# Key weights first on a second DMA queue, value weights fourth on the first, engine lists reordered and most filler matmuls dropped

The kernel is one pre-norm transformer block (linear attention, then a gated feed-forward), in bfloat16. It runs on one core of a Trainium2 chip. The metric is the device time of one execution in microseconds (us). Executions of one kernel differ: the kernel before took 208.06 to 208.45 us in its first four (0.2%). Names such as `wT`, `w2m`, `pp` and `vv` are those of the operations in the kernel's own order lists; PE is TensorE, DVE is VectorE, ACT is ScalarE, POOL is GpSimd, SP is SyncE.

## The reference

```python
# x: (1, 2048, 448), 16 heads of 28; everything bfloat16
def _A_ref(x, wqkv, w_phi, wo):
    qkv = (x @ wqkv).reshape(B, S, 3, H, Dh).transpose(2, 0, 3, 1, 4)
    q, k, v = qkv[0], qkv[1], qkv[2]
    pq = einsum("bhsd,hdf->bhsf", q, w_phi)
    pk = einsum("bhsd,hdf->bhsf", k, w_phi)
    phi_q = concatenate([softmax(pq), softmax(-pq)], -1)
    phi_k = concatenate([softmax(pk), softmax(-pk)], -1)
    kv = einsum("bhsf,bhsd->bhfd", phi_k, v)
    ...                                   # num, den, o = num / den
    return o.reshape(B, S, D) @ wo
h  = x + _A_ref(layernorm(x), wqkv, w_phi, wo)
h2 = h + (sigmoid(n @ w_gate) * (n @ w_up)) @ w_down        # n = layernorm(h)
```

`k` is only used through `w_phi`, so the kernel multiplies the key weights by `w_phi` once (the "fold": transpose the key weights on PE, `wT`; evacuate, that is, copy the result out of PE's accumulator; multiply, `w2m`; evacuate) and then projects x with the product (`pp`). The value projection (`vv`) needs no fold. `kv` is a sum over all 16 row tiles of x, so nothing after it can start before all tiles are through.

## The kernel before

Each engine runs a list of named operations in a fixed order; semaphores make an operation wait for what it reads. The order lists are the tuned part. The loads of the opening:

```python
def load(name, dst, src, w, kb, r=(), eng="sp"):
    return op(eng, name, lambda e: e.dma_start(dst, src), r=r, w=w, dma="in" if eng == "sp" else "ain", ...)
op("dve", "bd0", lambda e: e.memset(Wphi[:], 0.0), w=["Wphi"])
def kload(a, b):                                    # key weights, two halves of 196 KB
    load("ld_k%d" % a, wk_sb[:, a:b, :], A_wqkv[a * GP:b * GP, D:2 * D]..., (b - a) * 98)
for hl in range(4):                                 # w_phi: four loads into a block diagonal
    load("wphi%d" % hl, Wphi[hl * DH:(hl + 1) * DH, :, hl * DH:(hl + 1) * DH],
         A_w_phi...[hl], [("Wphi", hl)], 6, r=["Wphi"], eng="act")
# matmuls on zeros ("fillers"; "warm" in the lists): (how many, columns)
for i, (n, size) in enumerate(((9, 512), (1, 128), (5, 128), (1, 128), (8, 128), (9, 128), (9, 128), (3, 128))):
    op("pe", "warm%d" % i, warm(n, size), r=["zero"], w=[B(3)])
ORDER = {
  "sp":  "x1 x0 ld_k0 x2 ld_k2 x4 x6 ld_v0 x10 ld_v2 ld_q2 x8 ... xT12 xT13 xT14 ld_woo1 xT15 ld_wd0 ld_woe0 ld_wu2 ...",
  "act": "wphi3 wphi2 wphi1 wphi0 wTe1 wTe0 wTe3 w2e0_0 ...",
  "pe":  "warm0 wT1 wT0 warm1 xT1 warm2 xT0 warm3 wT2 wT3 w2m0_0 warm4 w2m0_1 w2m0_3 w2m0_2 warm5 xT2 warm6 "
         "ppa0 warm7 ppb0 xT3 vva0 vvb0 ppa2 ...",
  ...
}
```

Here `x1` and so on load tiles of x, `xT4` to `xT15` are DMA transposes of normalised tiles, `ld_wg`, `ld_wu`, `ld_wd`, `ld_wo` are the later weights.

The softmax here doesn't subtract the row's maximum and nothing guards it: scores larger than these inputs give would overflow.

Of the kernel before, what the change touches and what calls it, by code (L numbers as in the profile page):

```python
# [18 lines left out]
class Graph:  # L19
# [86 lines left out]
    def emit(self, nc):  # L106
# [94 lines left out]

ORDER = {
    "sp": (
        "x1 x0 ld_k0 x2 ld_k2 x4 x6 ld_v0 x10 ld_v2 ld_q2 x8 ld_q3 ld_q1 ld_q0 xT4 xT5 xT6 x14 x12 xT7 ld_woe1 xT8 "
        "xT9 xT10 xT11 xT12 xT13 xT14 ld_woo1 xT15 ld_wd0 ld_woe0 ld_wu2 ld_wg0 ld_wg2 ld_wd1 ld_wg3 ld_wu3 ld_woo0 "
        "ld_wu0 ld_wg1 ld_wd4 ld_wd6 ld_wu1 oT3 oT2 oT4 oT5 oT6 oT7 hT2 ld_wd3 ld_wd2 hT3 ld_wd5 hT4 oT8 oT9 hT5 hT6 "
        "hT7 oT11 oT10 oT12 out3 out1 hT9 hT8 oT13 hT11 hT10 oT14 oT15 out5 hT12 hT14 out2 hT15 out4 hT13 out9 out7 "
        "out10 out6 out14 out0 out15 out12 out11 out8 out13 "
    ),
    "act": (  # L210
        "wphi3 wphi2 wphi1 wphi0 wTe1 wTe0 wTe3 w2e0_0 w2e0_1 w2e0_2 w2e0_3 xn3 xn4 ek0 ek1 xn5 v1_0 v1_1 xn6 ek2 ek3 "
        "v1_2 w2e1_1 v1_3 xn7 ek4 w2e1_3 xn9 w2e1_2 ek5 v1_5 v1_6 ek6 xn11 ek7 xn12 ek8 v1_8 xn13 ek9 xn14 ek10 v1_10 "
        "ek11 v1_11 ek12 v1_12 ek13 v1_13 ek14 eq0_0 ek15 v1_14 v1_15 eq0_1 eq1_0 eq1_1 eq2_0 oT0e eq2_1 sq0 sq1 "
        "eq3_0 eq3_1 sig0_1 sig0_0 sig0_3 sig0_2 sig0_5 sig0_4 sig0_7 sq2 sig0_6 sq3 sig0_9 sig0_8 sig0_10 sig0_11 "
        "sq5 sig0_12 sig0_13 sq4 sq7 sig2_0 sig2_1 sq6 sig2_3 sig2_2 sig2_5 sig2_4 sig2_6 sig2_7 sig2_8 sig2_9 "
        "sig2_10 sig2_11 sig2_12 sig2_13 sig4_1 sq9 sig4_0 sig4_3 sq8 sig4_2 sig4_5 sig4_4 sig4_7 sig4_6 sig4_9 sq10 "
        "sig4_8 sq11 sig4_11 sig4_10 sig4_13 sig4_12 sig8_1 sig8_0 sq13 sig8_2 sig8_3 sig8_4 sig8_5 sq12 sig8_6 sq14 "
        "sq15 sig8_7 sig8_9 sig8_8 sig8_10 sig8_11 sig8_13 sig8_12 sig12_0 sig12_1 sig12_3 sig12_2 sig12_5 sig12_4 "
        "sig12_7 sig12_6 sig12_8 sig12_9 sig12_11 sig12_10 sig12_12 sig12_13 "
    ),  # L220
    "pe": (
        "warm0 wT1 wT0 warm1 xT1 warm2 xT0 warm3 wT2 wT3 w2m0_0 warm4 w2m0_1 w2m0_3 w2m0_2 warm5 xT2 warm6 ppa0 warm7 "
        "ppb0 xT3 vva0 vvb0 ppa2 ppb2 vva2 vvb2 kva0 w2m1_1 w2m1_0 kvb0 kva1 pva4 kvb1 pvb4 w2m1_3 w2m1_2 pva5 pva6 "
        "pvb5 pvb6 kva2 pqa0_0 kvb2 pva7 kva3 pvb7 pva8 kvb3 pvb8 pva9 kva4 pvb9 kvb4 pva10 kva5 pvb10 pva11 kvb5 "
        "kva6 pvb11 kvb6 pva12 kva7 pvb12 pva13 kvb7 pvb13 kva8 pva14 kvb8 kva9 pvb14 kvb9 pqb0_0 kva10 pva15 kvb10 "
        "kva11 pvb15 kvb11 kva12 pqa0_1 kvb12 kva13 pqb0_1 kvb13 kva14 pqa1_0 kvb14 kva15 kvb15 pqb1_0 pqa1_1 num0 "
        "num1 pqb1_1 pqa2_0 pqb2_0 num2 pqa2_1 oT0 pqb2_1 oT1 num3 woa0 wob0 pqa3_0 num4 pqb3_0 pqa3_1 pqb3_1 num5 "
        "hT0 hT1 ga0_1 gb0_1 ga0_0 num6 gb0_0 ga0_3 woa2 gb0_3 ga0_2 wob2 gb0_2 num7 ga0_5 gb0_5 ga0_4 gb0_4 ga0_7 "
        "gb0_7 ga0_6 num8 gb0_6 woa4 ga0_9 ga0_8 gb0_9 gb0_8 wob4 ga0_11 ga0_10 gb0_11 gb0_10 woa6 num9 wob6 ga0_13 "
        "ga0_12 gb0_13 gb0_12 dn0_0 dn0_4 ga2_0 ga2_1 gb2_0 gb2_1 dn0_8 dn0_11 ga2_3 num10 ga2_2 gb2_3 dp0_0 gb2_2 "  # L230
        "dp0_4 ga2_5 ga2_4 gb2_5 gb2_4 dp0_8 dp0_11 ga2_6 ga2_7 gb2_6 gb2_7 woa8 ga2_8 ga2_9 gb2_8 gb2_9 wob8 num11 "
        "ga2_10 ga2_11 gb2_10 gb2_11 dn2_0 ga2_12 ga2_13 gb2_12 gb2_13 dn2_4 dn2_8 ga4_1 num12 gb4_1 ga4_0 dn2_11 "
        "gb4_0 dp2_0 ga4_3 ga4_2 gb4_3 dp2_4 num13 gb4_2 ga4_5 dp2_8 gb4_5 ga4_4 dp2_11 gb4_4 ga4_7 num14 gb4_7 ga4_6 "
        "woa10 gb4_6 ga4_9 wob10 gb4_9 ga4_8 num15 gb4_8 ga4_11 woa12 gb4_11 ga4_10 wob12 gb4_10 ga4_13 dn4_0 ga4_12 "
        "gb4_13 gb4_12 dn4_4 ga8_1 ga8_0 gb8_1 gb8_0 dn4_8 dn4_11 ga8_3 ga8_2 dp4_0 gb8_2 dp4_4 dp4_8 gb8_3 ga8_4 "
        "dp4_11 gb8_4 ga8_5 woa14 gb8_5 ga8_6 wob14 gb8_6 ga8_7 dn6_0 gb8_7 dn6_4 ga8_8 ga8_9 dn6_8 gb8_9 gb8_8 "
        "dn10_0 dn6_11 ga8_11 ga8_10 gb8_11 gb8_10 dp6_0 dp6_4 dp6_8 ga8_13 ga8_12 gb8_13 gb8_12 dp6_11 dn10_4 dn10_8 "
        "ga12_0 ga12_1 gb12_0 dn8_0 dn10_11 gb12_1 ga12_2 dp10_0 ga12_3 dn8_4 gb12_3 gb12_2 dp10_4 dn8_8 ga12_5 "
        "dn8_11 ga12_4 gb12_5 gb12_4 dp8_0 dp8_4 ga12_7 ga12_6 gb12_7 dp10_8 dp10_11 gb12_6 dp8_8 dp8_11 ga12_9 "
        "ga12_8 gb12_9 gb12_8 dm14_0 dm12_0 dm15_0 ga12_11 ga12_10 gb12_11 gb12_10 dm12_4 dm14_4 dm13_0 ga12_12 "  # L240
        "ga12_13 gb12_12 gb12_13 dm15_4 dm14_8 dm15_8 dm12_8 dm15_10 dm14_10 dm14_12 dm14_13 dm15_12 dm12_10 dm12_12 "
        "dm15_13 dm12_13 dm13_4 dm13_8 dm13_10 dm13_12 dm13_13 "
    ),
    "dve": (
        "zero bd0 bst1 agg1 bst0 agg0 ve1_0 nm1_0 nm1_1 xn1 bst2 bst3 agg2 agg3 ve1_3 xT0e wTe2 bst5 nm1_3 bst4 agg5 "
        "agg4 bst6 xT1e ve1_4 bst7 agg7 agg6 bst10 xT2e bst11 agg10 xT3e nm1_6 ss0 agg11 rs0 ss1 bst8 rs1 bst9 agg8 "
        "ss2 agg9 ss3 w2e1_0 rs3 rs2 v1_4 bst15 bst14 bst13 ss4 agg14 agg13 bst12 rs4 agg15 agg12 xn10 ss5 ss6 v1_7 "
        "rs6 rs5 ss7 rs7 ss8 v1_9 ss9 rs9 rs8 xn15 ss10 ss11 rs11 rs10 ss12 rs12 ss13 phi11 ss14 rs13 rs14 phi13 ss15 "
        "rs15 phi15 kvz1 kvz0 rsm0 qq0 rsm1 b0 c0 qq1 den0 b1 rden0 c1 rsm2 den1 qq2 rden1 b2 c2 den2 oT1e rsm3 rden2 "
        "qq3 b3 c3 h0 den3 nm0 rden3 h1 rsm4 nm1 qq4 b4 c4 den4 hn0 hn1 rsm5 hT0e hT1e qq5 b5 c5 den5 rden4 hh0_1 "  # L250
        "rsm6 qq6 rden5 b6 hh0_0 c6 den6 rden6 hh0_3 h2 rsm7 hh0_2 qq7 b7 hh0_5 c7 nm2 hh0_4 den7 rden7 h3 nm3 rsm8 "
        "hh0_7 hh0_6 hn2 qq8 b8 hn3 hh0_9 hh0_8 h5 h4 nm5 c8 nm4 den8 hh0_10 hh0_11 rsm9 qq9 h6 h7 b9 c9 hh0_12 "
        "hh0_13 nm7 rden8 nm6 den9 hh2_0 hh2_1 hn4 rsm10 rden9 qq10 b10 hh2_3 c10 hh2_2 hn6 hn7 den10 hh2_5 hh2_4 "
        "fin0 fin1 hh2_6 hh2_7 hn5 rden10 hh2_8 hh2_9 h8 h9 hh2_10 hh2_11 rsm11 qq11 nm9 b11 hh2_13 c11 hh2_12 den11 "
        "rsm12 qq12 nm8 b12 c12 rden11 hh4_1 hh4_0 o10 den12 hh4_3 rsm13 qq13 b13 rden12 hh4_2 c13 hh4_5 den13 fin3 "
        "hn9 rden13 hh4_4 hn8 fin2 rsm14 hh4_7 o13 qq14 b14 c14 hh4_6 den14 h10 h11 nm10 hh4_9 nm11 rsm15 hn10 hh4_8 "
        "hn11 hh4_11 qq15 h13 h12 hh4_10 b15 c15 hh4_13 nm13 hh4_12 den15 nm12 rden15 o15 rden14 hh8_1 hh8_0 o14 "
        "hh8_2 hh8_3 fin4 fin5 hh8_4 hh8_5 h15 h14 nm14 hh8_6 nm15 hn12 hn14 hh8_7 hh8_9 hh8_8 hn13 hn15 hh8_11 "
        "hh8_10 hh8_12 hh8_13 fin6 fin7 hh12_0 hh12_1 hh12_3 hh12_2 hh12_5 hh12_4 hh12_7 fin11 hh12_6 fin9 fin10 fin8 "
        "hh12_8 hh12_9 hh12_11 hh12_10 hh12_12 hh12_13 fin14 fin15 fin12 fin13 "  # L260
    ),
    "pool": (
        "ident0 phipad wqpad mask0 neghalf ident ve1_1 pow1_1 pow1_0 xn0 v1ones mask1 nm1_2 ve1_2 pow1_2 nb1_2 xn2 "
        "pow1_3 nm1_4 nb1_3 pow1_4 nb1_4 ve1_6 opad0 mask2 pow1_6 nb1_6 phi0 phi1 nm1_8 ve1_8 pow1_8 nb1_8 xn8 phi2 "
        "phi3 ve1_12 nm1_12 pow1_12 kvzones nb1_12 phi4 phi5 phi6 phi7 phi8 phi9 phi10 phi12 phi14 o0 o1 o2 o3 ve0 "
        "pow2_0 ve1 pow2_1 o4 o5 o6 o7 ve2 pow2_2 ve3 pow2_3 ve5 ve4 pow2_4 o8 pow2_5 ve7 o9 ve6 pow2_7 pow2_6 ve8 "
        "ve9 o11 pow2_9 o12 pow2_8 ve10 pow2_10 ve11 pow2_11 ve12 pow2_12 ve14 pow2_14 ve15 ve13 pow2_15 pow2_13 "
    ),
}
PROGRAM = (  # L270
    "pq:0,0,4 pq:0,1,4 kvz pq:1,0,0 pq:1,1,4 pq:2,0,0 num:0 num:1 ot:0 ot:1 wo:0 pq:2,1,4 pq:3,0,0 num:2 num:3 "
    "wo:2 pq:3,1,4 gu:0,2 num:4 num:5 wo:4 gu:2,2 num:6 num:7 wo:6 down:0,2 num:8 num:9 wo:8 down:2,2 num:10 "
    "num:11 wo:10 gu:4,4 num:12 num:13 wo:12 down:4,2 num:14 num:15 wo:14 down:6,2 gu:8,4 down:8,2 down:10,6 "
    "gu:12,4 down1:12,2 down1:13,3 down1:14,6 down1:15,7 "
)



def windows(ap):
# [26 lines left out]
def build(nc, A_x, A_wqkv, A_w_phi, A_wo, B_w_gate, B_w_up, B_w_down, out):  # L306
# [10 lines left out]
    with ExitStack() as es:  # L317
# [3 lines left out]
        ident = sb("ident", [P, P])  # L321
        zero = sb("zero", [P, 512])
        neghalf = sb("neghalf", [P, 4], f32)
# [100 lines left out]

        def kload(a, b):
            load("ld_k%d" % a, wk_sb[:, a:b, :], A_wqkv[a * GP:b * GP, D:2 * D].rearrange("(kt p) n -> p kt n", p=GP),
                 [("wk", kt) for kt in range(a, b)], (b - a) * 98)

        def vload(k):
            r0 = ROW0[k]  # L430
            load("ld_v%d" % k, wv_sb[:, k:k + 2, :], A_wqkv[r0:r0 + 256, 2 * D:3 * D].rearrange("(kt p) n -> p kt n", p=P),
                 [("wv", k), ("wv", k + 1)], 224)
        kload(0, 2)
        kload(2, 4)
        for hl in range(4):
# [28 lines left out]
                    p = e.matmul(bk(3)[:, 0:size], lhsT=zero[:, 0:P], rhs=zero[:, 0:size], start=True, stop=True)  # L464
                return p
            return f
        for i, (n, size) in enumerate(((9, 512), (1, 128), (5, 128), (1, 128), (8, 128), (9, 128), (9, 128), (3, 128))):
            op("pe", "warm%d" % i, warm(n, size), r=["zero"], w=[B(3)])

        def evac(name, dst, src, rkey, wkey):  # L470
# [64 lines left out]
        for kt in range(KT):  # L535
            b = (0, 1, 4, 5)[kt]
# [351 lines left out]
```

## Time and profile before

| | before |
|---|---|
| time, median (lowest to highest) | 208.24 us (208.06 to 208.45, 4 runs) |
| PE busy, share of the span | 96% |
| first real projection (`ppa0`) starts | 10.59 us |
| `kv` sum masked (`kvz`, on DVE) starts | 46.27 us |

The first lines of the page give the span and each engine's busy time.

```profile
span 206.8 us, 5794 instructions
...
PE 199.2 (96%) x2457; PEld 112.6 (54%) x2457; DVE 136.6 (66%) x343; ACT 95.2 (46%) x185; POOL 59.0 (29%) x99
```

PE is busy 96% of the time, so it bounds the kernel; but part of that is work on zeros. The chain of waits, followed back from the end (start, length, what), says where the opening comes from.

```profile
2.17 3.85 DMA x_sb<-in_A_x_dram
...
9.76 0.40 PE psum L478 x4
10.16 0.50 PE psum L464 x9
10.66 0.86 PE psum L289 x8
```

It starts at a load of x (the tiles `x2`), and nine fillers stand in the chain at 10.16 us. The timeline of the opening (start, length, engine, line, operation, then in brackets how long the engine had been idle and what ended it) has the first statistics of x, the fold, fillers around it, and the first projection.

```profile
2.88 0.63 DVE L485 BATCH_NORM_STATS2 st<-x_sb 128x6 f32<-128x448 bf16 x1 [1.46 <-DMA x_sb<-in_A_x_dram]
...
6.54 0.52 PE L464 MATMUL psum<-zero 128*128 128x128 bf16 x5
...
7.59 0.36 PE L553 MATMUL psum<-Wphi,WkT 112*128 112x112 bf16 x4
...
7.79 0.61 PE L464 MATMUL psum<-zero 128*128 128x128 bf16 x8
...
9.99 0.67 PE L464 MATMUL psum<-zero 128*128 128x128 bf16 x9
...
10.59 0.93 PE L289 MATMUL psum<-Wk,xnT 64*128 64x448 bf16 x8
```

DVE's timeline of the kernel before, at `kvz`, in the same columns:

```profile
46.27 1.19 DVE L657 TENSOR_TENSOR kvz<-psum,maskK 120x464 bf16<-120x464 f32 x2 [1.01 <-PE psum L289]
```

### The profile page before, as it was taken

To read this page: it belongs to the slowest core of one execution; us is meant where nothing else is said; L and a number is where in the kernel's file an instruction comes from. 1 tells how busy PE (TensorE), PEld (TensorE's weight loads), DVE (VectorE), ACT (ScalarE), POOL (GpSimd) and SP (SyncE) were. 2 spreads that over 40 slices of the span, in tenths; PEclk is the share of its full clock that TensorE was granted. 3 is DMA by queue.
4 is the path that set the end of the run, shared out by engine and by line. 5 is a ranking of instruction groups with operands and counts; after the bars stand their busy time and mean duration, and the time that the engine had idled before them with its cause. 6 is when DMAs were issued, how large, how long until landed. Compare 5 with 4: busy or idle time off the path is not lost.

```text
span 206.8 us, 5794 instructions
## 1 busy us (share of the span) xinstructions
PE 199.2 (96%) x2457; PEld 112.6 (54%) x2457; DVE 136.6 (66%) x343; ACT 95.2 (46%) x185; POOL 59.0 (29%) x99
## 2 busy tenths in 40 slices
PE   7999999999989999999999999999999999999991
PEld 2935666775446666777444444444555555544450
DVE  4899999978899897767768967446332513353151
ACT  2689999878792536222333342324323122122100
POOL 4868999831345404400032020001400000000000
PEclk9999999999999999999999999999999999999997
DMA  5945344899122270413005411030321000020013
GB/s 156 292 107 135 82 95 88 247 382 258 56 51 54 44 166 32 79 25 55 3 0 91 109 29 25 15 41 22 78 49 25 3 0 3 0 89 3 0 37 119
DMA packets 32722, 16.25 MB, mean 79 GB/s; under 512 B 24952, under 2 KB 31800, under 8 KB 32696
## 3 DMA queue, kind: packets, MB, share of 16 engines
q1 hardware_dynamic: 32192, 15.86, 31.2%
q8 instruction: 19, 0.31, 0.6%
q10 hardware_dynamic: 504, 0.03, 0.2%
q14 instruction: 7, 0.06, 0.1%
HBM read 8.34 MB, written 1.84 MB: 49 GB/s over the span
## 4 chain that ended last, share of the span: by engine, by line
PE 86%; DVE 4%; POOL 3%; DMA 2%; issue 1%; ACT 1%; SPq 1%
PE psum L289 79%; PE psum L814 5%; DMA x_sb<-in_A_x_dram 2%; POOL o_pad L700 1%; PE psum L478 1%; POOL rst L728 1%; SPq L388 1%; DVE hn_pad L732 1%; DVE st L485 1%; ACT eq L637 0%; PE psum L553 0%; ACT eq L638 0%; POOL xn_pad L514 0%; PE psum L464 0%; DVE hhT L788 0%
## 5 line engine op out<-in xcount | busy, mean ns | idle before, releaser
L289 PE MATMUL psum<-xnT,wg_sb 64*128 64x512 bf16 (+1 forms) x490 | 94.6, 333 | 0.7 <-DVE qq L685 0.6
L289 PE MATMUL psum<-xnT,wu_sb 64*128 64x512 bf16 (+1 forms) x490 | 94.5, 334 | 0.3
L787 ACT ACTIVATE sg_sb<-psum 128x512 bf16<-128x512 f32 (+1 forms) x70 | 35.0, 512 | 89.9 <-PE psum L289 89.4
L788 DVE SCALAR_TENSOR_TENSOR hhT<-sg_sb,psum 128x512 bf16<-128x512 bf16 (+1 forms) x70 | 39.1, 576 | 50.8 <-ACT sg_sb L787 50.3
L289 PEld LDWEIGHTS psum<-xnT,wg_sb 64*128 64x128 bf16 x490 | 43.8, 94 | 23.7 <-DVE hhT L788 4.8
L289 PEld LDWEIGHTS psum<-xnT,wu_sb 64*128 64x128 bf16 x490 | 43.9, 94 | 15.1 <-PE psum L289 1.4
L289 PE MATMUL psum<-wd_sb,hhT 64*128 64x448 bf16 x336 | 37.2, 349 | 0.0
L289 PEld LDWEIGHTS psum<-wd_sb,hhT 64*128 64x128 bf16 x336 | 17.3, 94 | 14.8 <-DVE x_sb L718 0.6
L607 POOL TENSOR_TENSOR phi<-hhT,rs 128x896 bf16<-128x896 bf16 x13 | 22.7, 1770 | 2.6 <-DVE rs L604 1.5
L289 PE MATMUL psum<-wv_sb,xnT 64*128 64x448 bf16 x112 | 22.0, 350 | 0.1
L289 PE MATMUL psum<-Wk,xnT 64*128 64x448 bf16 x112 | 22.0, 350 | 0.1
L726 POOL TENSOR_SCALAR ve<-ssq 128x1 f32<-128x1 f32 x16 | 3.1, 192 | 61.2 <-ACT junk L723 60.4
L603 DVE TENSOR_REDUCE ss<-hhT 128x32 f32<-128x896 bf16 x16 | 17.0, 1070 | 1.2 <-ACT hhT L600 1.1
L700 POOL TENSOR_TENSOR o_pad<-c_sb,rden 128x448 bf16<-128x448 bf16 x12 | 11.2, 937 | 19.0 <-DVE rden L695 17.4
L289 PE MATMUL psum<-xnT,Wq 64*120 64x512 bf16 x112 | 14.7, 381 | 0.2
L289 PE MATMUL psum<-wo_e,oT 64*128 64x448 bf16 x56 | 13.2, 350 | 0.2 <-DVE oT L471 0.2
L289 PE MATMUL psum<-wo_o,oT 64*128 64x448 bf16 x56 | 13.2, 350 | 0.1
L289 PEld LDWEIGHTS psum<-v,phi 64*120 64x120 bf16 x256 | 10.9, 131 | 3.3 <-PE psum L289 0.2
L821 DVE SCALAR_TENSOR_TENSOR x_sb<-psum,x_sb 128x448 bf16<-128x448 f32 x16 | 9.4, 619 | 3.5 <-PE psum L814 3.1
L723 ACT ACTIVATE junk<-x_sb,nm 128x448 bf16<-128x448 bf16 x16 | 10.6, 663 | 2.2 <-DVE nm L721 2.1
L289 PE MATMUL psum<-v,phi 64*120 64x116 bf16 x256 | 11.1, 213 | 0.1
L814 PE MATMUL psum<-wd_sb,hhT 128*128 128x448 bf16 x56 | 11.1, 353 | 0.0
(82 smaller groups left out, 240.2 us busy)
## 6 DMA issues: line engine op xcount, KB each, us to landing
out_dram<-x_sb SPq DMA_DIRECT2D x16, 112.0 KB, 1.8
x_sb<-in_A_x_dram SPq DMA_DIRECT2D x7, 224.0 KB, 4.3
wd_sb<-in_B_w_down_dram SPq DMA_DIRECT2D x7, 224.0 KB, 4.1
wg_sb<-in_B_w_gate_dram SPq DMA_DIRECT2D x3, 448.0 KB, 6.6
wu_sb<-in_B_w_up_dram SPq DMA_DIRECT2D x3, 448.0 KB, 9.9
wv_sb<-in_A_wqkv_dram SPq DMA_DIRECT2D x2, 224.0 KB, 4.8
wk_sb<-in_A_wqkv_dram SPq DMA_DIRECT2D x2, 196.0 KB, 3.9
wo_e<-in_A_wo_dram SPq DMA_DIRECT2D x1, 336.0 KB, 3.4
```

What stands on the lines that cost most here:

```text
L289: p = e.matmul(o, lhsT=w, rhs=r, start=st, stop=sp, tile_position=(row, 0))
L388: return op(eng, name, lambda e: e.dma_start(dst, src), r=r, w=w, dma="in" if eng == "sp" else "ain", nring=48 if eng == "sp" else 8, kb=kb)
L478: p = e.transpose(ps[:, kt * P:(kt + 1) * P], src, ident[:])
L603: op("dve", "ss%d" % t, lambda e: e.tensor_reduce(ss[:, s, :], eks, AX.X, ALU.add), r=[("ek", s)], w=[("ss", s)])
L607: return e.tensor_tensor(phi[:, sp, :, :, :].rearrange("p a g (f n) -> p (a g f) n", f=2)[:, :, 0:56].rearrange("p b (h d) -> p b h d", h= ...
L700: return e.tensor_tensor(o_pad[:, so, off:off + D].rearrange("p (h d) -> p h d", h=H), c_sb[:, s, :, 0:DH], rden[:, s, :][:, :, None].to_b ...
L723: op("act", "sq%d" % t, lambda e: e.activation(junk[:, t % 2, :], h_sb[:, t, :], ACT.Square, bias=nm2[:, t:t + 1], accum_out=ssq2[:, t:t + ...
L726: op("pool", "ve%d" % t, lambda e: e.tensor_scalar(ve2[:, t:t + 1], ssq2[:, t:t + 1], 1.0 / D, EPS, op0=ALU.mult, op1=ALU.add), r=[("ssq2" ...
L787: op("act", "sig" + nm, lambda e: e.activation(sg_sb[:, k, 0:N], bk(bg)[:, 0:N], ACT.Tanh, scale=0.5), r=[B(bg)], w=[("sg", k)])
L788: op("dve", "hh" + nm, lambda e: e.scalar_tensor_tensor(out=hhT[(t0 // 4) % NHH][:, ff, ns], in0=sg_sb[:, k, 0:N], scalar=1.0, in1=bk(bu)[ ...
L814: p = e.matmul(bk(b)[:, 0:D], lhsT=hb[:, ff, TS(t)], rhs=wd_sb[:, ff, :], start=ff == 0, stop=ff == FT - 1)
L821: op("dve", "fin%d" % t, lambda e: e.scalar_tensor_tensor(out=h_sb[:, t, :], in0=bk(b)[:, 0:D], scalar=0.5, in1=h_sb[:, t, :], op0=ALU.mul ...
```

## The change

The intent: fetch the key weights as the very first thing on ScalarE's queue, so that SyncE's queue reaches x2 and the value weights earlier; let PE project values first, which need no fold; drop most fillers; and reorder every engine's list for the new landing times. The diff, cut to its core (the rest of these three lists, and those of DVE and POOL, were reshuffled throughout):

```diff
     "sp": (
-        "x1 x0 ld_k0 x2 ld_k2 x4 x6 ld_v0 x10 ld_v2 ld_q2 x8 ld_q3 ld_q1 ld_q0 xT4 xT5 xT6 x14 x12 xT7 ld_woe1 xT8 "
-        "xT9 xT10 xT11 xT12 xT13 xT14 ld_woo1 xT15 ld_wd0 ld_woe0 ld_wu2 ld_wg0 ld_wg2 ld_wd1 ld_wg3 ld_wu3 ld_woo0 "
+        "x1 x0 x2 ld_v0 ld_v2 x4 x6 x10 ld_q1 x8 ld_q2 ld_q3 ld_q0 xT4 x12 xT5 xT6 x14 xT7 ld_woo1 xT8 ld_wd5 xT9 "
+        "xT10 xT11 xT12 ld_wu1 xT13 ld_woe1 xT14 ld_wu2 xT15 ld_wd1 ld_wg0 ld_wg3 ld_woe0 ld_wd3 ld_woo0 ld_wu3 "
     ...
     "act": (
-        "wphi3 wphi2 wphi1 wphi0 wTe1 wTe0 wTe3 w2e0_0 w2e0_1 w2e0_2 w2e0_3 xn3 xn4 ek0 ek1 xn5 v1_0 v1_1 xn6 ek2 ek3 "
+        "ld_k0 ld_k2 wphi0 wphi1 wphi3 wphi2 wTe3 wTe1 wTe2 w2e0_0 xT0e w2e0_2 w2e0_3 w2e0_1 xn3 v1_1 xT2e v1_0 ek0 "
+        "ek1 v1_2 w2e1_1 xn6 w2e1_0 ek2 ek3 w2e1_2 w2e1_3 xn8 ek4 v1_4 xn9 ek5 xn10 ek6 v1_6 xn11 ek7 v1_7 ek8 v1_8 "
     ...
     "pe": (
-        "warm0 wT1 wT0 warm1 xT1 warm2 xT0 warm3 wT2 wT3 w2m0_0 warm4 w2m0_1 w2m0_3 w2m0_2 warm5 xT2 warm6 ppa0 warm7 "
-        "ppb0 xT3 vva0 vvb0 ppa2 ppb2 vva2 vvb2 kva0 w2m1_1 ...
+        "warm0 wT0 wT3 wT1 warm1 xT1 wT2 warm2 w2m0_0 warm3 xT0 w2m0_2 w2m0_3 w2m0_1 warm4 vva0 xT2 vvb0 ppa0 xT3 "
+        "ppb0 vva2 vvb2 w2m1_0 w2m1_1 ppa2 ppb2 w2m1_3 w2m1_2 kva0 ...
...
-                 [("wk", kt) for kt in range(a, b)], (b - a) * 98)
+                 [("wk", kt) for kt in range(a, b)], (b - a) * 98, eng='act')
...
-        for i, (n, size) in enumerate(((9, 512), (1, 128), (5, 128), (1, 128), (8, 128), (9, 128), (9, 128), (3, 128))):
+        for i, (n, size) in enumerate(((9, 512), (2, 128), (3, 128), (3, 128), (2, 128))):
```

## The prediction

> **What bounds it.** TensorE. The page shows PE busy 199.2 of 206.8 us, and the chain of waits is 86% PE. The table of windows has PE idle about 0.5 us in all before 45 us, and 0.1 to 1.1 us per window from 45 to 80 us. But some of it is filler: the groups view up to 46 us has 45 warm-up matmuls on zeros (L464), 7.4 us: nine of 512 columns (4.02 us, 447 ns each[...]) and 36 of 128 columns (3.3 us in the timeline), which fill the opening's waits until 11.8 us.
>
> **Why the opening waits.** The chain starts with the x2 load: issued at 2.17 us as SyncE's fourth DMA, landed 6.02; statistics, rstd and normalisation take until 9.72, its transpose until 10.16. The key weights land at about 5.2 us (first half) and 7.1 us (second half, issued 2.67), so the fold with w_phi runs 7.5 to 9.05 us, its evacuations end at 10.1, and the first real projection starts at 10.6. The value weights, issued at 4.11 and 5.10, land at 9 to 10 us.
>
> **What the change does.** (a) Two key loads of 0.42 us issue each go to ScalarE's queue, which waited until 1.45 us for a memset; x2 moves up about 0.5 us, value weights 2 to 2.5, the second key half about 1.5. [...] DMA share 0.9 to 1.1 from 2 to 12 us. The bytes up to x2 and the keys stay about 840 KB, so I expect x2 at 5.5 to 6.2, hardly earlier. (b) Value projections of tiles 0 and 1 go ahead of the key ones; they need no fold, so they fill PE time that fillers had. (c) Small fillers fall from 36 to 10: about 2.4 us less. (d) One phi (1.09 us) more on VectorE, two transposes' and one fold's evacuation (0.4 to 0.6 us each) less; ACT nearly even.
>
> **How much is on the path.** Ceiling 2.4 us, the fillers. Against it: x2 hardly moves, so 0.3 to 0.8 us of bare waiting appears where fillers stood; and from 20 to 40 us VectorE (19.4 of 20 us busy), GpSimd (19.1) and ScalarE (18.5) are almost full, so part of PE's earlier start may be given back. First real projection at about 8.5 us; end of projections (kvz evacuation, 46.3 us now) 1.7 us earlier. After that the same work in another order: 0, give or take 0.6 us, mainly at 50 to 75 us where weights and the attention chain meet. Tail unchanged.
>
> **Predicted:** 206.6 us (1.7 us, 0.8% less), 8 in 10 between 205.4 and 207.9. Faster by over 2%: 4%; within 2%: 94%; slower: 2%.
>
> **Right if** the groups show 19 warm matmuls of about 5 us; value projections start first, at 8 to 9 us; kvz starts 1.7 us earlier; the difference is there by 46 us and stays.
> **Wrong if** wv lands after 9 us or x2 is pushed behind the keys (fillers come back as idle PE); if GpSimd's phi or VectorE's reductions set the pace from 20 to 45 us; if the reordered weight loads delay the first gate/up matmuls (61.1 us now) or slow the xT transposes[...].

The sum came to 206.6 us: 208.24 less the 1.7 us expected at `kvz`, and 0 after it. The nine fillers of 512 columns start 427 ns apart, the 512-column matmuls of the feed-forward, in pairs, 212 to 216 ns, and the DMA share was 0.90 to 1.10 in each 2 us from 2 to 12 us.

## More of the kernel before

From 6 to 10 us PE is bare for only 0.20 us; the waits are stuffed with 36 small fillers. In SyncE's own timeline the transposes of x follow each other, with only one small weight load (`ld_woo1`, 56 KB, at 33.62 us) before the last one:

```profile
22.28 11.30 SPq L524 DMA_TRANSPOSE xnT<-xn_pad  x7
33.62 0.59 SPq L388 DMA_DIRECT2D wo_o<-in_A_wo_dram  x1
34.26 1.27 SPq L524 DMA_TRANSPOSE xnT<-xn_pad  x1
```

## The result and the profile after

| | before | after |
|---|---|---|
| time, median (lowest to highest) | 208.24 us (208.06 to 208.45) | 209.17 us (209.12 to 209.44) |
| small fillers | 36 | 10 |
| first real projection starts | 10.59 us | 10.04 us |
| `kvz` starts | 46.27 us | 47.19 us |
| first gate/up matmul (`ga0_1`) starts | 61.09 us | 62.02 us |

The changed kernel is 0.9 us slower: ratio 1.0047, 95% interval 1.0029 to 1.0064. (Ratios here are the mean time of one kernel's fast runs over that of the other's in the same rounds, so they are not quite the ratio of the quoted medians. By the 2% rule every kernel below is simply "same".) The first gate/up matmul carries the whole difference, and so does `kvz`: the loss is made before 47 us. The last matmuls end 0.55 us later, so 0.4 us of it comes back in the feed-forward.

The chain of the changed kernel has two DMA waits in it that the chain before had not:

```profile
3.27 4.90 DMA Wphi<-in_A_w_phi_dram
...
8.53 0.36 PE psum L554 x4
...
10.04 0.93 PE psum L290 x8
...
30.80 5.55 DMA xnT<-xn_pad
...
36.49 9.42 PE psum L290 x168
```

PE's own waits up to 48 us in the kernel before:

```profile
PE psum L464 <- DVE zero L392: 1.2, 1, 1.2
PE psum L478 <- POOL xn_pad L514: 0.2, 1, 0.2
```

The same view of the changed kernel:

```profile
PE psum L554 <- DMA Wphi<-in_A_w_phi_dram: 1.3, 1, 1.3
PE psum L465 <- DVE zero L393: 1.2, 1, 1.2
PE psum L290 <- DMA xnT<-xn_pad: 0.7, 1, 0.7
```

And the same stretches of the table of windows (stretch and its length, then busy time and instructions of PE, PE's weight loads, DVE, ACT and POOL; then the granted clock of PE, the DMA share and GB/s) in the kernel before:

```profile
6.00:8.00 2.00, 2.00 (x34) 2.00 (x33) 1.92 (x7) 1.05 (x3) 1.46 (x6) 1.00 1.05 337
8.00:10.00 2.00, 1.80 (x34) 1.56 (x32) 2.00 (x8) 2.00 (x5) 1.81 (x4) 1.00 1.10 266
34.00:36.00 2.00, 2.00 (x34) 1.31 (x30) 1.97 (x3) 1.63 (x4) 2.00 (x2) 1.00 0.48 105
36.00:38.00 2.00, 2.00 (x44) 1.49 (x42) 1.88 (x5) 1.71 (x4) 2.00 (x2) 1.00 0.65 159
```

The windows of the changed kernel:

```profile
6.00:8.00 2.00, 1.23 (x18) 1.06 (x16) 1.93 (x7) 1.50 (x3) 1.78 (x4) 1.00 1.10 345
8.00:10.00 2.00, 1.46 (x25) 1.31 (x25) 1.50 (x5) 1.08 (x3) 1.66 (x6) 1.00 1.13 234
34.00:36.00 2.00, 1.83 (x38) 1.24 (x32) 2.00 (x3) 1.87 (x5) 1.53 (x2) 1.00 1.09 93
36.00:38.00 2.00, 1.51 (x22) 1.09 (x24) 2.00 (x4) 1.06 (x3) 2.00 (x2) 1.00 1.05 204
```

Between 6 and 10 us PE stands bare for 4.00 - 1.23 - 1.46 = 1.31 us, where before it was 0.20; between 34 and 38 us for 0.66, where before it was 0. The timeline says what it stood for. The opening of the changed kernel:

```profile
3.60 0.63 DVE L486 BATCH_NORM_STATS2 st<-x_sb 128x6 f32<-128x448 bf16 x1 [2.17 <-DMA x_sb<-in_A_x_dram]
...
8.53 0.36 PE L554 MATMUL psum<-Wphi,WkT 112*128 112x112 bf16 x4 [1.29 <-DMA Wphi<-in_A_w_phi_dram]
...
10.04 0.93 PE L290 MATMUL psum<-wv_sb,xnT 64*128 64x448 bf16 x8
```

DVE's timeline of the changed kernel, at `kvz`:

```profile
47.19 1.19 DVE L658 TENSOR_TENSOR kvz<-psum,maskK 120x464 bf16<-120x464 f32 x2 [1.01 <-PE psum L290]
```

SyncE's own timeline of the changed kernel, with the two loads and the transpose in question:

```profile
30.02 0.73 SPq L389 DMA_DIRECT2D wu_sb<-in_B_w_up_dram  x1
30.80 1.19 SPq L525 DMA_TRANSPOSE xnT<-xn_pad  x1
...
34.11 0.59 SPq L389 DMA_DIRECT2D wu_sb<-in_B_w_up_dram  x1
```

Three readings.

1. **The fold waits for w_phi, not for the keys.** The keys land early, as meant, and their transposes are done at 7 us. The four small w_phi loads, now behind the keys, are issued by 3.70 us and land at 8.18 us. In the trace's packet records the last w_phi packet ends at 6.69 us before and at 7.48 us after. Before, the fold began at 7.59 us: w_phi had at most 0.9 us to spare (an estimate: 0.2, if its landing came 0.7 us after the last packet, as it did after the change). No wait showed it, because until then PE was busy with fillers and transposes that stand ahead of the fold in its list.
2. **x1 lands later too.** The first statistics wait until 3.60 us instead of 2.88, with 392 KB of keys now issued beside it. Two later runs show that the keys are the cause: with the keys alone moved (e7) it is 3.92 us, with the keys moved back (e2) 2.91. In e3, where the keys are issued only 0.45 us later on the same queue, it is 3.02, so that edit frees x1 as well as w_phi.
3. **A transpose of x waits among weights.** `xT13` is issued at 30.80 us, right behind the 448 KB of `ld_wu1` (30.02 us), and PE gets its tile at 36.35 us, 5.5 us later; the median such transpose took 3.0 us in this kernel and 2.5 us before.

An account from the starts of PE's instructions closes the sum. From the first filler to the last `kv` matmul, take for each operation the time until the next one starts. The stretches that belong to fillers, with the waits behind them, are 6.75 us before and 6.15 us after: 26 fillers less bought 0.6 us, because the w_phi wait moved into their place. (Counted like this, the 36 small ones took 2.76 us before; the ten that are left take 2.34 us, waits included.) All other operations together took 1.5 us more than before beyond the usual time of their kind: 0.8 us of it is the `xT13` wait, most of the other 0.7 us are three small waits from 17.5 to 18.6 us (the second fold and the first `kv` product). The net is the 0.9 us of `kvz`. So the opening did not lose time against the kernel before, it only failed to gain: the first projection starts 0.55 us earlier. The loss is made after it.

### The profile page after: what moved, and what is told of

It is laid out like the page before. It is cut to its first block, busy times and chain, and to the rows that moved or that the text cites. A ratio compares the mean times of both kernels' runs of the same rounds, so it can differ in the third digit from the quotient of the medians.

```text
span 207.4 us, 5743 instructions
## 1 busy us (share of the span) xinstructions
PE 197.5 (95%) x2431; PEld 110.1 (53%) x2431; DVE 137.2 (66%) x340; ACT 94.8 (46%) x186; POOL 60.6 (29%) x101
## 4 chain that ended last, share of the span: by engine, by line
PE 83%; DMA 5%; DVE 3%; POOL 2%; ACT 2%; issue 1%; ACTq 1%; POOLq 0%
PE psum L290 77%; PE psum L815 5%; DMA xnT<-xn_pad 3%; DMA Wphi<-in_A_w_phi_dram 2%; ACTq L389 1%; PE psum L479 1%; ACT xn_pad L512 1%; PE psum L554 1%; POOL rst L729 1%; DVE xnT L472 1%; DVE st L486 1%; POOL o_pad L701 0%; POOL rst L499 0%; DVE b_sb L688 0%; DVE c_sb L691 0%
## 5 line engine op out<-in xcount | busy, mean ns | idle before, releaser
L290 PEld LDWEIGHTS psum<-xnT,wg_sb 64*128 64x128 bf16 x490 | 44.4, 94 | 24.1 <-DVE hhT L789 4.6
L290 PEld LDWEIGHTS psum<-xnT,wu_sb 64*128 64x128 bf16 x490 | 44.4, 94 | 15.0 <-PE psum L290 0.7
L290 PE MATMUL psum<-wd_sb,hhT 64*128 64x448 bf16 x336 | 37.8, 349 | 0.0
L290 PEld LDWEIGHTS psum<-wd_sb,hhT 64*128 64x128 bf16 x336 | 16.3, 94 | 15.8 <-DVE x_sb L719 0.3
L608 POOL TENSOR_TENSOR phi<-hhT,rs 128x896 bf16<-128x896 bf16 x12 | 20.5, 1725 | 2.0 <-PE psum L290 2.0
L701 POOL TENSOR_TENSOR o_pad<-c_sb,rden 128x448 bf16<-128x448 bf16 x11 | 10.6, 960 | 32.4 <-DVE rden L696 32.2
L724 ACT ACTIVATE junk<-x_sb,nm 128x448 bf16<-128x448 bf16 x16 | 10.6, 663 | 5.5 <-DVE nm L722 5.3
L290 PEld LDWEIGHTS psum<-v,phi 64*120 64x120 bf16 x256 | 10.3, 131 | 3.4 <-PE psum L290 0.6
L486 DVE BATCH_NORM_STATS2 st<-x_sb 128x6 f32<-128x448 bf16 x16 | 9.4, 614 | 2.8 <-DMA x_sb<-in_A_x_dram 2.7
```

Of the source, the lines that this page charges most:

```text
L290: p = e.matmul(o, lhsT=w, rhs=r, start=st, stop=sp, tile_position=(row, 0))
L486: op("dve", "bst%d" % t, lambda e: e.bn_stats(st1[:, t, :], x_sb[:, t, :]), r=[("x", t)], w=[("st1", t)])
L608: return e.tensor_tensor(phi[:, sp, :, :, :].rearrange("p a g (f n) -> p (a g f) n", f=2)[:, :, 0:56].rearrange("p b (h d) -> p b h d", h= ...
L701: return e.tensor_tensor(o_pad[:, so, off:off + D].rearrange("p (h d) -> p h d", h=H), c_sb[:, s, :, 0:DH], rden[:, s, :][:, :, None].to_b ...
L724: op("act", "sq%d" % t, lambda e: e.activation(junk[:, t % 2, :], h_sb[:, t, :], ACT.Square, bias=nm2[:, t:t + 1], accum_out=ssq2[:, t:t + ...
```

## The experiments

Theories, as they were put before the runs: **W**, the fold is held by w_phi behind the keys; **T**, transposes of x are held by weight loads queued between them; **V** (rival), DVE and POOL set the pace up to `kvz`, so holes in PE cost nothing; and after the first runs **C**, a guess from e1's profile (full rate lost at 9.22 us, after a bare wait of 1.8 us, for 3.41 us): a bare wait of PE in the first 10 us costs PE's clock. "Changed kernel" is the kernel after. Each kernel was compared with the kernel before on the same chip (its median was 208.40 to 208.56).

| run | median | lowest to highest | ratio to before (95%) |
|---|---|---|---|
| e1 transposes first | 208.52 | 208.43 to 210.12 | 1.0016 (0.9992 to 1.0040) |
| e2 keys back on SyncE | 210.52 | 208.79 to 211.28 | 1.0090 (1.0055 to 1.0125) |
| e3 w_phi in one load, first | 209.37 | 208.65 to 210.18 | 1.0043 (1.0016 to 1.0070) |
| e4 = e1 + e3 | 209.12 | 207.83 to 209.68 | 1.0020 (0.9992 to 1.0048) |
| e5 = e4 + filler | 208.16 | 207.88 to 208.32 | 0.9982 (0.9970 to 0.9994) |
| e6 reordered | 207.56 | 207.20 to 207.93 | 0.9956 (0.9942 to 0.9970) |
| e7 before, keys on ScalarE's queue | 209.06 | 208.95 to 209.22 | 1.0027 (1.0015 to 1.0040) |
| e8 before, few fillers | 207.93 | 207.88 to 208.63 | 0.9982 (0.9968 to 0.9995) |
| e9 w_phi second on SyncE | 211.04 (210.98 without the slow one) | 209.42 to 211.60, and 719.28 | 1.0103 (1.0072 to 1.0133) |
| e10 = e9 + all reorderings | 210.54 | 210.12 to 211.22 | 1.0096 (1.0078 to 1.0115) |
| e11 changed kernel again | 209.48 | 208.81 to 209.98 | 1.0039 (1.0020 to 1.0059) |
| e12 e6, one evacuation earlier | 207.41 | 207.22 to 207.93 | 0.9946 (0.9930 to 0.9962) |
| e13, e14, e15: e4, single looks (state unknown) | 209.21, 209.12, 208.20 | | |
| e16 e1 + filler in the wait | 208.67 | 208.36 to 208.93 | 1.0006 (0.9991 to 1.0021) |

### e1: transposes ahead of the weights

```diff
-  "... xT8 ld_wd5 xT9 xT10 xT11 xT12 ld_wu1 xT13 ld_woe1 xT14 ld_wu2 xT15 ld_wd1 ..."
+  "... xT8 xT9 xT10 xT11 xT12 xT13 xT14 xT15 ld_wd5 ld_wu1 ld_woe1 ld_wu2 ld_wd1 ..."
```

> The changed kernel, but the four weight loads that it put between the transposes of normalised x (wd5, wu1, woe1, wu2) are issued after the last of these transposes. Theory T (transposes queued among weight loads): the 0.66 us wait of PE at 36 us, 'DMA xnT<-xn_pad', is gone, kvz starts 0.6 to 1.0 us earlier than 47.2 us, and the time falls by 0.6 to 1.0 us to about 208.3. Rival V (VectorE, busy 98% from 14 to 38 us, and GpSimd's phi set the pace until kvz; holes in PE cost nothing): the wait goes but kvz moves by under 0.3 us.

The wait at 36 us is gone, and five of six executions took 208.43 to 208.69 us, 0.5 to 0.8 us less than the changed kernel's usual 209.2: T holds as a time. The expected shift of `kvz` can't be read in e1, whose one profile was slowed by something else (see below), but e16 below, which has the same order of transposes (and eleven fillers more), has it: `kvz` at 46.68 us, 0.5 us earlier than the changed kernel's 47.19, and a ratio of 1.0006 (0.9991 to 1.0021), clear of the changed kernel's 1.0047 (1.0029 to 1.0064). So as a time, undoing T takes back nearly the whole loss. `kvz` is then still 0.4 us later than in the kernel before (46.27 us); the feed-forward wins that back, as it does in the changed kernel. In e11, the changed kernel again, the same stretch had only 0.11 us of idle PE, so the size of this term differs between executions. The remaining execution of e1, the profiled one, took 210.12 us, and its table of windows shows something new in the column after POOL, the granted clock:

```profile
8.00:10.00 2.00, 1.28 (x18) 1.31 (x19) 1.81 (x7) 0.89 (x2) 1.69 (x6) 0.80 1.10 306
10.00:12.00 2.00, 2.00 (x18) 1.08 (x15) 2.00 (x6) 2.00 (x5) 1.55 (x5) 0.50 0.73 155
```

PE ran at half rate (granted clock 0.50 from 10 to 12 us) in the middle of the opening. In the clock records of the trace full rate comes at 5.81 us, is taken away at 9.22 and comes back at 12.63, 3.41 us later. Half of 3.41 us is 1.7 us (an estimate of the loss at a clock of 0.50), close to the 1.6 us that this execution took beyond the median of the others. It had waited bare for w_phi for 1.8 us just before. That is where theory C comes from.

### e2: keys back on SyncE's queue

```diff
-  sp: "x1 x0 x2 ld_v0 ..."              act: "ld_k0 ld_k2 wphi0 ..."
+  sp: "x1 x0 ld_k0 x2 ld_k2 ld_v0 ..."  act: "wphi0 ..."
```

> The changed kernel, but with the key loads back on SyncE's queue (places 3 and 5, as before), w_phi alone on ScalarE's. Theory W (the fold waits for w_phi, which the keys ahead of it on the same queue delay): w_phi lands about 0.8 us earlier, the 1.29 us wait at 8.5 us shrinks to under 0.6, and the time falls by 0.3 to 0.8 us although the keys land 1 to 1.5 us later. If instead early keys are worth what the change meant: 0.5 to 1.5 us slower than the changed kernel.

A miss as a time: the median is 1.3 us over the changed kernel's, with 2.5 us between the fastest and the slowest execution. The profile is of the fastest one (208.79 us). In it the fold starts at 8.13 instead of 8.53 us and w_phi is no longer waited for, but the second key half is, until 6.66 us. A gain for W is not shown by it: the changed kernel itself had an execution of 208.81 us with `kvz` at 46.85 (e11), against 46.84 here. As a time, e2 falls in the range of the rival in its expectation, 0.5 to 1.5 us slower because early keys are worth something, and speaks against W. Why the other executions are up to 2.5 us slower was not seen in a profile; that it is the clock is argued from e13 to e15, not shown. The recorded mean clocks do not settle it: 0.991, 0.991 and 0.997 in the three slowest.

### e3 and e4: w_phi out of the way

One load of w_phi into a scratch tile, which need not wait for the memset, and a masked copy on POOL:

```diff
-        for hl in range(4):
-            load("wphi%d" % hl, Wphi[hl * DH:..., :, hl * DH:...], ..., r=["Wphi"], eng="act")
+        load("wphi0", wtmp[:], A_w_phi.rearrange("(g hl) i j -> (hl i) g j", hl=4), ["wtmp"], 25, eng="act")
+        ...                                          # wm: 112 x 4 mask, 1 where row p is in block hl
+        op("pool", "wphim", lambda e: e.tensor_tensor(Wphi[:]..., wtmp[:]...to_broadcast([GP, G, 4, DH]),
+            wm[:]...to_broadcast([GP, G, 4, DH]), ALU.mult), ...)
-  act: "ld_k0 ld_k2 wphi0 wphi1 wphi3 wphi2 wTe3 ..."
+  act: "wphi0 ld_k0 ld_k2 wTe3 ..."
```

> The changed kernel, but w_phi comes by one DMA, first on ScalarE's queue, into a scratch tile without waiting for the memset, and GpSimd spreads it into its block diagonal with a mask; the keys follow on the same queue. Theory W: w_phi is ready before 5 us, the 1.29 us wait at 8.5 us goes, the fold starts at about 7.2 us, the first real projection at 8.8 to 9.2 instead of 10.04, and kvz starts 0.8 to 1.3 us earlier. Rival V: the first projection comes earlier all the same but kvz moves by 0.5 us at most. The wait at 36 us stays under both.

> Both edits together. Theories W and T together: the gains add, 1.4 to 2.2 us less than the changed kernel, about 207.2 us, which beats the kernel before by about 1 us. Rival V: less than 0.7 us together.

In e3's profile w_phi is there at 3.33 us (and spread by 4.26), as expected, and the wait for it is gone:

```profile
3.33 0.93 POOL L443 TENSOR_TENSOR Wphi<-wtmp,wm 112x448 bf16<-112x448 bf16 x1 [0.92 <-DMA wtmp<-in_A_w_phi_dram]
```

And the waits of the same kernel e3 up to 48 us, the one for the keys:

```profile
PEld psum L549 <- DMA wk_sb<-in_A_wqkv_dram: 1.5, 2, 0.9
```

Yet the fold starts at 8.53 us, to the hundredth as in the changed kernel. The keys, issued 0.5 us later, have their last packet 1.0 us later (5.60 against 4.57 us); PE gets the second half at 6.41 us, and now waits for it. Both expectations failed: no gain from e3, and e4 spreads from 207.83 to 209.68 us. In both profiles the same small matmuls also take longer: the twelve last `w2m` took 0.85 us (e3) and 0.83 us (e4) in the chain, against 0.59 in that of the changed kernel. By the clock records the array came to full rate only at 10.26 us (e3) and 10.38 us (e4), against 6.55 us.

### e5: a filler where e4 waits

```diff
-  pe: "warm0 wT0 wT3 wT1 warm1 ..."
+  pe: "warm0 wT0 warm1 wT3 wT1 warm2 ..."       # the new warm1: ten matmuls of 128 columns
```

> e4 with one more filler of ten 128-column matmuls on zeros between the transposes of the first and the second key half, where e4's PE waited about 0.9 us for the keys. Theory C (clock: [...] e4's runs lay between 207.8 and 209.7 us for that reason): more work makes it faster, the first rise of the clock is before 8 us instead of 10.6, no run over 208.6, median 207.6 to 208.2. If the spread is not the clock's: median and spread of e4 (209.1) stay, or get 0.2 us worse.

More work made it faster: 208.16 against 209.12 us (on another chip; in ratio to the kernel before 0.9982 against 1.0020, with intervals that overlap by a hair), and the executions lie within 0.44 us instead of 1.85. Full rate comes at 7.12 us. (The "10.6" of this expectation and the "10.68" of e13 count from 0.3 us before the profile's zero; on the profile's scale it is 10.38.)

### e13 to e15: one kernel, four executions

The kernel is e4, unchanged.

> e4 again, one execution with its profile, to set its time beside the moment of its first rise to full rate. Theory C: a time of 207.8 to 208.3 goes with a rise before 8 us, a time of 209.0 to 209.7 with one after 10 us (209.15 us and 10.68 us in the profile in hand); no theory says which it will be.

> As e13, another execution of e4: early rise (before 8 us) with 207.8 to 208.3 us, or late rise (after 10 us) with 209.0 to 209.7.

> As e13, another execution of e4: early rise (before 8 us) with 207.8 to 208.3 us, or late rise (after 10 us) with 209.0 to 209.7.

| execution of e4 | time | full rate from (clock records) |
|---|---|---|
| first | 209.15 | 10.38 us |
| e13 | 209.21 | 10.61 us |
| e14 | 209.12 | 4.06 us, taken away 7.47, back 10.89 |
| e15 | 208.20 | 4.53 us, kept |

The one execution that had full rate early and kept it was 0.9 to 1.0 us faster, and `kvz` has the same difference: 46.35 us in e15, 47.26 to 47.34 in the three others. These are four single executions, so the link is strong but rests on one fast case. The size, 0.5%, is as much as the whole effect, and it makes single runs misleading. The expectation knew two cases; e14 is a third (early rise, then taken away), with the time of the late rise. The key transposes and the last three quarters of the fold show it. The windows of e14:

```profile
6.00:8.00 2.00, 1.28 (x19) 1.28 (x20) 1.69 (x6) 0.83 (x2) 1.72 (x3) 0.87 1.08 346
8.00:10.00 2.00, 2.00 (x23) 1.98 (x21) 1.83 (x7) 1.61 (x4) 1.63 (x6) 0.50 1.11 288
10.00:12.00 2.00, 2.00 (x22) 1.16 (x19) 2.00 (x6) 2.00 (x5) 1.43 (x6) 0.78 0.85 188
```

PE's timeline of e14 (start, length, engine, line, operation, then the idle time before it):

```profile
6.72 0.62 PE L549 MATMUL psum<-ident,wk_sb 112*112 112x112 bf16 x8 [1.41 <-DMA wk_sb<-in_A_wqkv_dram]
...
9.35 1.33 PE L562 MATMUL psum<-Wphi,WkT 112*128 112x112 bf16 x12
```

The same lines of PE's timeline of e15:

```profile
6.88 0.62 PE L549 MATMUL psum<-ident,wk_sb 112*112 112x112 bf16 x8 [1.17 <-DMA wk_sb<-in_A_wqkv_dram]
...
8.95 0.76 PE L562 MATMUL psum<-Wphi,WkT 112*128 112x112 bf16 x12
```

The same twelve matmuls take 1.33 us in one and 0.76 us in the other. Before both, PE had waited bare for the first key half (0.17 and 0.34 us) and for the second (1.41 and 1.17 us), so the waits alone do not tell why only e14 lost its rate. The stretch at half rate lasted 3.42 us in e14 (7.47 to 10.89) and 3.41 us in e1. A warning for the reader of such a page: in e4 and e13 the column shows 1.00 in every window before the first clock record (10.38 and 10.61 us), although three small fillers took 0.53 us there (at 8.36 and 8.22 us), as in e14 at a granted clock of 0.50, against 0.33 us in e15 after its rise. The late rise shows only in the lengths of known matmuls and in the clock records.

### e16: a filler in the w_phi wait of e1

```diff
-  ... enumerate(((9, 512), (2, 128), (3, 128), (3, 128), (2, 128)))
+  ... enumerate(((9, 512), (2, 128), (14, 128), (3, 128), (2, 128)))
```

> e1 with 14 instead of 3 small fillers just before the fold, in PE's wait of 1.3 to 1.8 us for w_phi. Theory C: the array no longer falls back to half rate after that wait (in e1's profile it did at 9.2 us, for 3.4 us, and that execution took 210.12 us): no execution over 209.0, median 208.4 to 208.6 as in the five others of e1. If fillers are work on the path: about 0.8 us slower, 209.3.

No execution over 208.93 us, full rate from 5.46 us on, median 208.67. Eleven fillers more cost nothing that could be measured (e1's five normal executions had 208.43 to 208.69), so they were not on the path; a single slow execution in e1 is little to prove that they prevent, and e5 is the stronger evidence.

### e7 and e8: parts of the change, alone, in the kernel before

```diff
 e7
-  sp: "x1 x0 ld_k0 x2 ld_k2 x4 ..."   act: "wphi3 wphi2 ..."
+  sp: "x1 x0 x2 x4 ..."               act: "ld_k0 ld_k2 wphi3 wphi2 ..."
 e8
-  ((9, 512), (1, 128), (5, 128), (1, 128), (8, 128), (9, 128), (9, 128), (3, 128))
+  ((9, 512), (1, 128), (1, 128), (1, 128), (1, 128), (1, 128), (1, 128), (1, 128))
```

> The kernel before with the two key loads, alone, put first on ScalarE's queue; all else as before. If early keys are worth time: 0.3 us or more faster. Theory W: the keys land 1 to 1.8 us earlier, but w_phi lands about 0.8 us later than its 7.0 us and now ends the wait before the fold, so the fold starts at 8 to 8.5 us instead of 7.6; the first projection is some 0.3 to 0.7 us later, and the time is 0 to 0.7 us longer.

> The kernel before with its 36 small fillers cut to 7, all else as before. The prediction's ceiling took the fillers' 2.4 us as time that could be given back. Theory: they stand in waits that end with data, so at best under 0.3 us is gained; theory C adds that some or all executions get 0.5 to 1.7 us slower[...], with a spread of over 1 us between runs against 0.9 us of the kernel before.

e7: the named part of the change, alone, costs time: 209.06 against 208.40 us. The fold starts at 8.38 instead of 7.59 us, as W had it. But the chain of this profile goes through x, not through w_phi:

```profile
3.92 0.63 DVE L485 BATCH_NORM_STATS2 st<-x_sb 128x6 f32<-128x448 bf16 x1 [2.50 <-DMA x_sb<-in_A_x_dram]
```

x1's statistics start at 3.92 instead of 2.88 us, and the delay runs through normalisation and transposes to `kvz` at 46.86 us, 0.59 us later than before. No wait of PE for w_phi shows in e7's profile. So the size was right, but by a route other than the one expected, which is in part luck: e7 shows that early keys cost time in the kernel before, not that they do it through w_phi.

e8: cutting 29 fillers, alone, gains 0.47 us by the medians (by the interval of the ratio 0.1 to 0.7), where under 0.3 was expected, and `kvz` starts at 45.60 us, 0.67 earlier. The fold starts at 6.94 us instead of 7.59, so the fillers were in part on the path. The feared slow executions did not come (207.88 to 208.63; full rate at 4.41 us in the profile). Theory C is not a law that every bare wait is punished: PE stood bare 0.47 us from 6 to 8 us and 1.14 us from 8 to 10 us there and kept its rate, and in e11 it kept it through a single wait of 1.69 us.

Multiplied, e7 (1.0027), e8 (0.9982) and the undoing of e1 (1.0047 / 1.0016, or 1.0039 / 1.0016 with e11) give 1.0040 or 1.0032: most of the measured 1.0047 and 1.0039. That is a check of consistency and no proof: the measured ratio is on both sides, so it says only that e1 (1.0016) and e7 times e8 (1.0009) agree, with intervals of 0.0013 to 0.0024 on either side.

### e9 and e10: w_phi ahead of x0

```diff
-  sp: "x1 x0 x2 ..."          act: "ld_k0 ld_k2 wphi0 ..."
+  sp: "x1 wphi0 x0 x2 ..."    act: "ld_k0 ld_k2 wTe3 ..."       # e10 adds the orders of e1 and e6
```

> The changed kernel with w_phi by one DMA (scratch tile and mask as in e3), issued second on SyncE's queue; the keys stay first on ScalarE's queue where the change put them, so unlike e3 they do not land later; no filler added. Theory W in its first form (w_phi alone held the fold): the 1.29 us wait at 8.5 us goes, fold at 7.2 to 7.6 us, kvz 0.7 to 1.2 us earlier than the 47.2 of the changed kernel, time 0.7 to 1.2 us less than e11. If e3 showed the rule (what stands ahead only hands the wait to the next load, x0 or x2 or the second key half): under 0.4 us less.[...]

> e9 with the transposes of x ahead of the weight loads (as e1), the two transposes of the first key half and their evacuation ahead, tile 0's transpose and evacuation ahead of the fold's, and the query fold's evacuation ahead of tile 6's normalisation. If the terms found so far add: 207.0 to 207.6 us. If it is over 208, something else holds the opening.

Both failed clearly, at 210.98 (the five fast executions) and 210.54 us. W in its first form ("w_phi alone") is dead as a repair; as a test of w_phi alone the edit is not clean, since it also delays x. In e10's profile the 25 KB of w_phi, issued second, arrive no earlier than 5.32 us, beside the keys, and x0 behind them is late by 1 us (x2 by 1.8, its statistics at 7.97 us instead of 6.17). PE has full rate from 6.57 us on and keeps it, and `kvz` starts at 48.28 us, so here late x, and not the clock, goes with the loss:

```profile
5.32 0.93 POOL L443 TENSOR_TENSOR Wphi<-wtmp,wm 112x448 bf16<-112x448 bf16 x1 [2.90 <-DMA wtmp<-in_A_w_phi_dram]
5.57 0.63 DVE L494 BATCH_NORM_STATS2 st<-x_sb 128x6 f32<-128x448 bf16 x1 [1.05 <-DMA x_sb<-in_A_x_dram]
```

In e3 and e10 the load that was moved ahead handed its wait to the next one: to the second key half in e3 (used at 6.41 us, and now waited for), to x0 in e10 (1 us late). e9's first execution, the profiled one, took 719.28 us. Its matmuls took 933 ns instead of 334 while DVE's instructions kept their length (580 ns against 576), and the trace has no clock record at all:

```profile
L290 PE MATMUL psum<-xnT,wg_sb 64*128 64x512 bf16 (+1 forms) x490 | 337.3, 933 | 0.6 <-issue 0.6
...
L797 DVE SCALAR_TENSOR_TENSOR hhT<-sg_sb,psum 128x512 bf16<-128x512 bf16 (+1 forms) x70 | 40.2, 580 | 353.7 <-ACT sg_sb L796 353.7
```

Start to start, matmuls of 512 columns stood 840 ns apart against 212 in the changed kernel, which is a quarter of the rate there. This execution is left out of the ratios. The other five had 209.42 to 211.60 us.

### e6 and e12: the version that beats both

e6 is e4 with PE's first transposes limited to the first key half, a filler of six where PE then waits for x, and the query fold's evacuation earlier on ScalarE:

```diff
-  pe:  "warm0 wT0 wT3 wT1 warm1 xT1 wT2 warm2 w2m0_0 ..."
+  pe:  "warm0 wT0 wT1 warm1 xT1 warm2 wT3 wT2 warm3 w2m0_0 ..."    # warm1: six of 128 columns
-  act: "wphi0 ld_k0 ld_k2 wTe3 wTe1 wTe2 ... w2e1_1 xn6 w2e1_0 ..."
+  act: "wphi0 ld_k0 ld_k2 wTe1 wTe3 wTe2 ... w2e1_1 w2e1_0 xn6 ..."
```

e12 also puts `xT0e` ahead of `w2e0_0` on ScalarE.

> A candidate: e4, with the two transposes that need only the first key half ahead, a filler of six small matmuls where PE waits for x, and the evacuation of the query fold ahead of the normalisation of tile 6 on ScalarE. If w_phi, the transposes among the weights, the evacuation order and the clock are the whole of what ate the gain: fold starts at 7.3 to 7.8 us, first projection at about 9, 207.0 to 207.6 us, under the kernel before by 0.4 to 0.7%. If VectorE or GpSimd set the pace to 46 us: not under 208.0.

> e6 with the evacuation of tile 0's transpose ahead of the first of the fold's on ScalarE; in e6 the first projection (9.43 us) began when that evacuation ended. If so it starts 0.3 to 0.5 us earlier and the time is 207.1 to 207.4; if the key projections then wait for the fold's last evacuation instead, no change (207.6).

e6 took 207.56 us: 0.44% under the kernel before, 0.8% under the changed one in ratio. Its first projection starts at 9.43 us (9 was expected) and `kvz` here:

```profile
45.97 1.19 DVE L666 TENSOR_TENSOR kvz<-psum,maskK 120x464 bf16<-120x464 f32 x2 [1.01 <-PE psum L290]
```

V had said "not under 208.0" and falls: with PE's waits removed, `kvz` did move. Which of e6's edits did it is not separated. One did not: the second fold, which the earlier evacuation was to speed up, took 1.31 us in e6 as in the changed kernel (1.00 in the kernel before), counted by PE's starts; its waits only moved. e12 is not told apart from e6 (0.9946 against 0.9956, overlapping intervals); in its one profile the first projection was not earlier (9.60 us), because that execution waited 0.9 us for the second key half. So the step that it was to test is open.

### e11: the control

> The changed kernel itself, as the control of these runs: 1.0047 times the kernel before, 209.2 us, within 0.4 us.

1.0039: the loss is real and repeats. In its profile, which is of its fastest execution (208.81 us), the w_phi wait is 1.7 us, the `xT` wait 0.1 us, and `kvz` starts at 46.85 us.

## Why the prediction was wrong

It said 206.6 us (205.4 to 207.9), 0.8% faster; the kernel took 209.17 us, 0.5% slower in ratio. Two steps failed. The first is the opening: it was to bring the first projection 2.1 us forward (10.6 to 8.5), and brought 0.55 us, because its path to the fold left out w_phi. The second is the way from there to `kvz`: of the gain, 0.4 us was to be given back (2.1 us down to 1.7), to VectorE, GpSimd and ScalarE; in fact 1.5 us were lost (from 0.55 us earlier to 0.92 later), about half of it in a transpose of x among weight loads. Point by point:

- **"PE bounds the kernel; part of it is filler."** Right. The loss is found in what PE did before 47 us; of e6's gain (0.6 us in the profiled execution), 0.30 us is seen in `kvz`.
- **"x2 at 5.5 to 6.2, hardly earlier."** Right; its statistics start at 6.17 us. The DMA share was 0.88 to 1.13 in each 2 us from 2 to 12 us, and the keys' gain was paid by x1 (2.88 to 3.60 us; 3.92 in e7) and by w_phi (6.69 to 7.48 us).
- **"First real projection at about 8.5 us."** Wrong: 10.04. The step behind it listed what moves up (x2, value weights, second key half) and never asked what moves back. It took the keys as the only gate of the fold, since PE's weight loads were seen to wait for them. w_phi stood right behind, and no wait in the profile could show that. Nor need the second key half's 7.1 us have been its landing: the trace shows only that PE came to it then, after fillers, and in e8, with few fillers, PE used it at 6.53 us.
- **"0.3 to 0.8 us of bare waiting appears where fillers stood."** This is the mis-sized term: it was 1.1 us more from 6 to 10 us (1.31 against 0.20). Of the "2.4 us ceiling" the account from PE's starts leaves 0.6. Also e8 shows what the fillers alone were worth in the kernel before: 0.47 us by the medians.
- **"1.7 us earlier at `kvz`; after that the same work in another order: 0, give or take 0.6."** The part after `kvz` is right: the kernel is 0.92 us behind there and 0.55 at the last matmul. The part before it is wrong. It counted on full engines from 20 to 40 us, and the runs showed a wait that it gave no number: +0.8 us at 36 us in the profile, from weight loads between the transposes. "Slow the xT transposes" stood in the list of what could go wrong; the new order had it in plain sight (`xT12 ld_wu1 xT13 ld_woe1 xT14 ld_wu2 xT15`). e1 measured it: about 0.6 us by the medians, and 0.5 us of `kvz` in e16.
- **PE's clock** was on the list of what could go wrong too. It is not what made the changed kernel slow (its two profiles have full rate from 6.55 and 5.72 us on; its other eight executions were not seen). But late full rate (10.26 us in e3, 10.38 in e4) goes with the two repairs that showed no gain, and with a filler it came at 7.12 us and the gain with it (e5).

What stays open: why e2 is so slow in most executions; which of the reordered lists causes the small waits at 17.5 to 18.6 us (e6's edit did not remove them); what the values-first order and the lists of DVE and POOL are worth, since no run has either of them alone; and what exactly decides whether a bare wait costs the clock.

## What to carry to other kernels

Before moving a load ahead, list everything it passes (here x1 became 0.72 us later and w_phi 0.8 us) and everything that waits at the same gate: the second-latest input, here w_phi, showed no wait before, then took over with one of 1.29 us. Keep latency-critical small transfers out from between bulk weight loads (here a transpose behind 448 KB took 5.5 us, against a median of 3.0). Filler work in a wait that must be there anyway was cheap here (e16: 208.67 against e1's 208.52 us), and with it full rate came early and stayed (7.12 us in e5, 5.46 us in e16); after removing it, look at single executions and at the lengths of known matmuls, not at one profile.
